# Attention with decay, then an FFN, on one core: the order of instructions planned inside the kernel

## The chip, the core and the metric

The kernel runs on one core of a Trainium2 chip. TensorE (PE) multiplies matrices into PSUM, VectorE (DVE) and ScalarE (ACT) work element by element, GpSimd (POOL) does so in SBUF only, and SyncE (SP) issues nearly all DMAs; each engine takes its instructions in a fixed order and waits on semaphores. The metric is the device time of one execution, in microseconds (us).

## The reference

```python
def _attn_ref(q, k, v, f):              # 8 batches, 8 heads, 576 positions, 64 wide
    scores = q @ k^T / sqrt(D)
    cum = np.cumsum(np.log(np.clip(f, 0.0001, 1.0)), axis=-1)
    scores = np.where(causal, -1e9, scores + cum[:, :, :, None] - cum[:, :, None, :])
    attn = softmax(scores)              # max, exp, divide by the sum + 1e-9
    return attn @ v
def _moe_ref(x, w_in, w_out):           # 4608 tokens, 512 -> 2048 -> 512
    h = x @ w_in
    g = np.where(h >= 1, h, np.where(h <= -1, 0.0, (h + 1) ** 2 / 4))
    return g @ w_out
```

x is the attention's output, with the heads of a position side by side. All data is float32.

## The kernel before

**Numbers in two halves.** A float32 operand of a large matmul is scaled by a power of two and split into two fp16 parts, high (`[.., 0, ..]`, written by ACT) and low (the rest, written by DVE, some by POOL). A product takes three fp16 matmuls: high by high, high by low, low by high. The scores pack both halves of q and k into the 128 rows and take two. The first jobs use plain float32 matmuls instead: scores up to job `NQK` = 12, values up to job `NPE` = 5.

**Jobs.** A job is a pair of heads of a batch. Batch 0 is cut in rows 0 to 255 and 256 to 575 (jobs 0 to 3 and 4 to 7), every other batch has four jobs of 576 rows; 36 in all, and 32 full pairs. Jobs 8 to 11 are batch 1, jobs 12 to 35 the 24 pairs of batches 2 to 7, which I number as pairs too (job 12 is the first). A job goes row block by row block (r = 0 to 4, 128 rows each, 64 in the last, where both heads share one tile):
- `load`, `prepare`: q and k come in; from job 12 on they are scaled and split into `qs` (L393 to L420, L420 once a pair), and a DMA transposes `qs` into `qkT`. Earlier jobs are transposed on PE (L375).
- `scores`: PE multiplies (L479 float32, L485 fp16), POOL makes the decay part from `ck` (the sums `cum_d`, broadcast to all rows) in `sdr` (four buffers) or `sd` (fifth row, two buffers) and masks it.
- `weights`: DVE adds both and takes the row's maximum (L572), ACT takes exp with the sum (L576), DVE inverts the sum, ACT and DVE write the high and low half of the weights (`pr`, L590 and L596), and SP's DMAs transpose `pr` into `pT` (L602, L605), of which there is one buffer. Up to job 4, `turn_rows` transposes on PE in float32 instead (L514, L520), with the inverse sums on a diagonal (L503).
- `values`: PE multiplies `pT` by v (L616, in float32 L545), in one run of 36 matmuls per pair, and ACT and DVE write x in two halves (L625, L626).

**v.** `split_values` loads a pair's v for its own values. Before that `value_scale` loads all of a batch's v once more, pair by pair through the `ck` buffers, for one maximum over the batch (L243 the load, L244 the reduce on DVE).

**FFN.** 18 chunks of 256 tokens by 8 blocks of the hidden width make 144 units. `moe_front` is 24 matmuls into a PSUM bank `ph` (L658, two banks), then ACT relu (L667) and square (L668), DVE max/min (L669), ACT high half (L671), DVE low half (L672); `moe_back` is 12 matmuls of 512 columns into `po` (L686). A chunk over a batch border has twice as many, narrower front matmuls. The FFN's weights arrive packed in pairs of words, are put right and split block by block in 32 pieces of 512 columns (`weight_split`, L195 to L227) during the first jobs.

**What sets the order.** The code is written job by job with quotas of FFN units in between; the framework's scheduler then orders the instructions by its own model of their times.

Of the kernel before, what the change touches and what calls it, by code (L numbers as in the profile page):

```python
# [25 lines left out]

CUTS = {0: ((0, 2), (2, 5))}

NPE = 5
NQK = 12  # L30

POOL_LOW = {6: (2, 4), 7: (2, 4)}

EARLY = ((0, 0, 3), (0, 3, 6), (0, 6, 8))

CONVERT = {1: 1, 2: 1, 3: 1, 4: 2, 5: 2, 6: 1}
LOADS = {0: 2, 1: 3}
# [9 lines left out]
def kernel(  # L47
# [10 lines left out]

# [35 lines left out]
    early = xpool.tile([P, NPAIR, 2, S], F16, name="x").rearrange("p a b s -> p (a b s)").bitcast(F32)  # L94

    xs = {b: xpool.tile([P, NPAIR, 2, S], F16, name="x") for b in range(2)}
    x1 = xs[1].rearrange("p a b s -> p (a b s)").bitcast(F32)
    stage = xs[1].rearrange("p a b s -> p (a b s)").bitcast(F32)
# [12 lines left out]

    def across(dst, m):

        n = m.shape[1]
        pt = ps.tile([P, 512], F32, name="s")
        nc.tensor.transpose(pt[0:n, 0:P], m, ident)  # L120
# [12 lines left out]

    ident = const.tile([P, P], F32, name="ident")
    make_identity(nc, ident)
    ones = const.tile([2, P], F32, name="ones")
    nc.gpsimd.memset(ones, 1.0)
    cum_d = dram.tile([B * H, S], F32, name="cum_d")
    cq = const.tile([P, NT5, B * H], F32, name="cq")

    def decay_sums():
        fl = early
        nb = B * H
        nc.sync.dma_start(fl[0:nb, 0:S], f.rearrange("b h s -> (b h) s"))
# [23 lines left out]
    wi = [place[2 * i].rearrange("p l (t c) -> p l t c", t=NKT) for i in range(NB)]  # L170
    wo = [place[2 * i + 1].rearrange("p l (t c) -> p l t c", t=2) for i in range(NB)]
    mi = const.tile([P, NB], F32, name="mi")
    mp = const.tile([P, 2, NB], F32, name="mp")
    sw = const.tile([P, 2, NB], F32, name="sw")

    def weight_load(i):
# [4 lines left out]
        for k_, slot in enumerate(RAW[i]):  # L181
            src = srcs[k_ // 2]
            n = src.shape[1] // 2
            nc.sync.dma_start(
                slots[slot].rearrange("p (t c) -> p t c", t=n), src[:, n * (k_ % 2):n * (k_ % 2 + 1), :]
            )

    def weight_split(i):
        ms = tiny.tile([P, 2, 2], F32, name="ms", bufs=2)
        wfs = []  # L190
        for k_, slot in enumerate(RAW[i]):
            top = slots[slot][:, 1::2]
            low = slots[slot][:, 0::2]
            bits = two.tile([P, DM], F32, name="u").bitcast(I32)
            nc.vector.tensor_scalar(  # L195
                out=bits, in0=top, scalar1=0x07FFFFFF, scalar2=3, op0=ALU.bitwise_and, op1=ALU.logical_shift_left
            )
            nc.vector.scalar_tensor_tensor(
                out=bits, in0=low, scalar=29, in1=bits, op0=ALU.logical_shift_right, op1=ALU.bitwise_or
            )  # L200
            nc.vector.scalar_tensor_tensor(
                out=top, in0=top, scalar=-0x40000000, in1=bits, op0=ALU.bitwise_and, op1=ALU.bitwise_or
            )
            wf = top.bitcast(F32)
            wfs.append(wf)
            m = ms[:, k_ // 2, k_ % 2:k_ % 2 + 1]
            if k_ < 0:
                nc.vector.tensor_reduce(out=m, in_=wf, axis=AX.X, op=ALU.max, apply_absolute_value=True)
            else:
                nc.scalar.activation(low.bitcast(F32), wf, AF.Abs, accum_out=m)  # L210
        m1 = tiny.tile([P, 2], F32, name="m1w", bufs=2)
        nc.vector.tensor_reduce(out=m1, in_=ms, axis=AX.X, op=ALU.max)
        m = tiny.tile([P, 2], F32, name="m2", bufs=2)
        across(m, m1)
        nc.vector.tensor_copy(mi[:, i:i + 1], m[:, 0:1])
        scale_of(sw[:, :, i], mp[:, :, i], m)
        for k_, wf in enumerate(wfs):
            j = k_ // 2
            s = sw[:, j, i:i + 1]
            c = slice(k_ % 2 * DM, (k_ % 2 + 1) * DM)  # L220
            hi, lo = place[2 * i + j][:, 0, c], place[2 * i + j][:, 1, c]
            nc.scalar.activation(hi, wf, AF.Copy, scale=s)
            if k_ < 2:
                nc.gpsimd.tensor_scalar(out=wf, in0=wf, scalar1=s, scalar2=0.0, op0=ALU.mult, op1=ALU.add)
                nc.gpsimd.tensor_tensor(out=lo, in0=wf, in1=hi, op=ALU.subtract)
            else:
                nc.vector.scalar_tensor_tensor(out=lo, in0=wf, scalar=s, in1=hi, op0=ALU.mult, op1=ALU.subtract)  # L227


    mv = const.tile([P, B], F32, name="mv")  # L230
    pv = const.tile([P, B], F32, name="pv")
    sv = const.tile([P, B], F32, name="sv")
    bsc = {}

    def value_scale(b):
        m4 = tiny.tile([P, NPAIR], F32, name="m4", bufs=2)
        for i in range(NPAIR):
# [5 lines left out]
            nc.sync.dma_start(st, part)  # L243
            nc.vector.tensor_reduce(  # L244
# [6 lines left out]
        if b:  # L251
            nc.vector.tensor_tensor(out=m, in0=m, in1=mv[:, b - 1:b], op=ALU.max)
# [590 lines left out]
```

## Time and profile before

| | us |
|---|---|
| median of three runs (1189.17 to 1194.98) | 1193.62 |
| span of the profiled execution (its whole time stands in no view; the median of the runs is 3.9 longer) | 1189.7 |
| PE busy | 1059.5 |
| VectorE busy | 816.9 |
| ScalarE busy | 804.5 |
| GpSimd busy | 452.7 |

The span runs from the first to the last instruction. Matmuls are pipelined and their modelled ends overlap, so the busy times of single lines of PE add up to more than PE's own. In a row of a view, "x" is the number of instructions, then come busy us and mean ns, and behind the bar the idle time of the engine before them with what ended it.

### The profile page before, as it was taken

The page shows a single profiled execution, that of the slowest core. Times are in us where ns is not written, and L with a number is a line of the kernel's source. Part 1 is how long each engine was busy: PE and PEld are TensorE (multiplying, and loading weights), DVE is VectorE, ACT ScalarE, POOL GpSimd, SP SyncE. Part 2 cuts the span into 40 slices and gives each one's busy share as a digit, 9 for nine tenths or more (in the row PEclk, how much of TensorE's full clock was granted, in tenths as well). Part 3 has the DMA queues.
Part 4 walks back from the last instruction along what each step waited for, and adds up shares of the span by engine and source line. Part 5 has one row for each costly group of instructions (what it writes and reads, how often), then busy time and mean ns, then how long its engine had stood idle before and what let it go on. Part 6 is the DMA issues. An engine that isn't in the chain of part 4 may idle for free. (4 is left out here: it accounts for less than half of the span.)

```text
span 1189.7 us, 24378 instructions
## 1 busy us (share of the span) xinstructions
PE 1059.5 (89%) x8553; PEld 695.6 (58%) x8553; DVE 816.9 (69%) x2327; ACT 804.5 (68%) x1698; POOL 452.7 (38%) x699
## 2 busy tenths in 40 slices
PE   4667788994889899999998999989898989999998
PEld 3444455662555566666665666656665656677665
DVE  6898886674877787778666868768866788523222
ACT  5867677773777687768775767758866687644443
POOL 5677453441554245425423225524533265000000
PEclk9778798997999999999999999999999999999999
DMA  8885466686899588968866649767978587300000
GB/s 261 251 232 134 114 144 131 132 149 137 152 161 191 110 173 158 184 137 170 168 105 134 128 85 172 153 148 149 168 134 173 116 169 110 74 19 2 18 19 18
DMA packets 439258, 160.04 MB, mean 135 GB/s; under 512 B 414944, under 2 KB 415968, under 8 KB 439136
## 3 DMA queue, kind: packets, MB, share of 16 engines
q1 hardware_dynamic: 433952, 149.05, 62.2%
q10 hardware_dynamic: 5184, 9.44, 2.4%
q8 instruction: 67, 1.10, 0.4%
q14 instruction: 55, 0.45, 0.1%
HBM read 75.64 MB, written 9.58 MB: 72 GB/s over the span
## 5 line engine op out<-in xcount | busy, mean ns | idle before, releaser
L658 PE MATMUL ph<-x,place 128*128 128x256 f16 (+3 forms) x4608 | 448.9, 248 | 30.1 <-DVE u L669 29.8
L658 PEld LDWEIGHTS <-place 128*128 128x128 f16 x4608 | 362.4, 99 | 117.0 <-issue 25.8
L686 PE MATMUL po<-place,g 128*128 128x512 f16 x1728 | 418.0, 380 | 7.5 <-DVE g L672 3.8
L686 PEld LDWEIGHTS <-g 128*128 128x128 f16 x1728 | 162.1, 98 | 169.2 <-ACT g L671 6.9
L489 POOL TENSOR_SCALAR sdr<-ck,nsig,cqs 128x128 f32<-128x128 f32 (+1 forms) x192 | 160.7, 840 | 214.7 <-DVE pr L596 142.6
L669 DVE SCALAR_TENSOR_TENSOR u<-ph,z,u 128x512 f32<-128x512 f32 x136 | 101.1, 744 | 109.8 <-ACT u L668 109.5
L576 ACT ACTIVATE sdr<-sdr,nm 128x384 f32<-128x384 f32 (+1 forms) x248 | 137.9, 557 | 49.3 <-DVE nm L572 44.0
L667 ACT ACTIVATE u<-ph,z 128x512 f32<-128x512 f32 x136 | 104.3, 767 | 80.2 <-PE ph L658 79.6
L596 DVE SCALAR_TENSOR_TENSOR pr<-sdr,rc,pr 128x384 f16<-128x384 f32 (+2 forms) x232 | 128.8, 580 | 30.2 <-ACT pr L590 29.9
L671 ACT ACTIVATE g<-u,z 128x512 f16<-128x512 f32 x136 | 97.3, 716 | 68.2 <-DVE u L669 66.1
L672 DVE SCALAR_TENSOR_TENSOR g<-u,z,g 128x512 f16<-128x512 f32 x136 | 105.1, 773 | 53.8 <-ACT g L671 53.4
L489 POOL TENSOR_SCALAR sd<-ck,nsig,cqs 64x576 f32<-64x576 f32 x48 | 53.8, 1120 | 222.6 <-DMA ck<-cum_d 84.3
L590 ACT ACTIVATE pr<-sdr,rc 128x384 f16<-128x384 f32 (+1 forms) x236 | 119.7, 556 | 14.6 <-DVE rc L587 5.0
L572 DVE CUSTOM_DVE_ANT_0 sdr<-s,sdr,nalpha 128x128 f32<-128x128 f32 (+1 forms) x192 | 102.1, 543 | 31.8 <-POOL sdr L493 18.2
L616 PE MATMUL big<-pT,vs 128*64 128x64 f16 (+3 forms) x1098 | 88.3, 285 | 30.0 <-DMA pT<-pr 28.4
L616 PEld LDWEIGHTS <-vs 128*64 128x64 f16 x1098 | 59.1, 111 | 65.8 <-issue 26.5
L493 POOL TENSOR_SCALAR_AFFINE_SELECT sdr<-sdr 128x128 f32<-128x128 f32 x248 | 91.7, 380 | 11.1
L668 ACT ACTIVATE u<-u 128x512 f32<-128x512 f32 x144 | 89.5, 622 | 2.0
L485 PE MATMUL s<-qkT 128*128 128x128 f16 (+3 forms) x384 | 78.4, 300 | 5.5 <-DVE nm L572 4.3
L393 ACT ACTIVATE qs<-qk 128x640 f16<-128x640 f32 x48 | 35.0, 729 | 58.4 <-DMA qkT<-qs 50.6
L485 PEld LDWEIGHTS <-qkT 128*128 128x128 f16 (+1 forms) x576 | 45.0, 101 | 39.9 <-issue 18.0
L489 POOL TENSOR_SCALAR sdr<-ck,cq 128x384 f32<-128x384 f32 (+3 forms) x56 | 44.8, 800 | 56.6 <-DVE pr L596 27.0
(168 smaller groups left out, 1175.0 us busy)
## 6 DMA issues: line engine op xcount, KB each, us to landing
ck<-cum_d SPq DMA_DIRECT2D x64, 288.0 KB, 4.1
out_dram<-ot ACTq DMA_DIRECT2D x36, 256.0 KB, 3.4
qk<-in_k_dram SPq DMA_DIRECT2D x64, 128.0 KB, 3.1
ck<-in_v_dram SPq DMA_DIRECT2D x28, 288.0 KB, 2.9
v<-in_v_dram SPq DMA_DIRECT2D x62, 128.0 KB, 3.5
qk<-in_q_dram SPq DMA_DIRECT2D x56, 128.0 KB, 2.6
place<-in_moe_w_in_dram SPq DMA_DIRECT2D x11, 512.0 KB, 5.3
place<-in_moe_w_out_dram SPq DMA_DIRECT2D x10, 512.0 KB, 6.0
```

The costliest lines, as they stand in the source:

```text
L485: nc.tensor.matmul(sp[p0:p1, c0:c1], lhsT=w.q[:, h, q0 - w.s0:q0 - w.s0 + p1 - p0], rhs=w.k[:, c, h, c0:c1], start=(c == 0), stop=(c == 1),)
L489: nc.gpsimd.tensor_scalar(out=sd[p0:p1, 0:wid], in0=w.ck[h][p0:p1, 0:wid], scalar1=w.nsig if w.p < NQK else w.nsig[p0:p1], scalar2=w.cqs[p ...
L572: nc.vector.tensor_tensor_reduce(out=a, in0=sp[:, 0:wid], in1=a, scale=w.nalpha, scalar=BIG, op0=ALU.add, op1=ALU.min, accum_out=nm[:, i:i ...
L576: nc.scalar.activation(a, a, AF.Exp, bias=nm[:, i:i + 1], scale=-1.0, accum_out=sm[:, i:i + 1])
L590: nc.scalar.activation(pr[:, :, 0, i, :], a, AF.Copy, scale=rc[:, i:i + 1])
L596: nc.vector.scalar_tensor_tensor(out=pr[:, :, 1, i, :], in0=a, scalar=rc[:, i:i + 1], in1=pr[:, :, 0, i, :], op0=ALU.mult, op1=ALU.subtract,)
L616: nc.tensor.matmul(av[64 * h:64 * h + 64, at + s0:at + s1], lhsT=w.vs[:, vl, h, t, :], rhs=w.pT[:, t, pl, h, s0:s1], start=(t == 0 and pi ...
L658: nc.tensor.matmul(ph[:, fi, a0:a1], lhsT=wi[fb][:, wl, t, fi * P:(fi + 1) * P], rhs=xs[b][:, t, xl, s0:s0 + a1 - a0], start=(fi == 0 and ...
L667: nc.scalar.activation(u, h, AF.Relu, scale=z.u[:, i:i + 1], bias=z.h[:, i:i + 1])
L669: nc.vector.scalar_tensor_tensor(out=u, in0=h, scalar=z.t[:, i:i + 1], in1=u, op0=ALU.max, op1=ALU.min)
L672: nc.vector.scalar_tensor_tensor(out=g[:, 1], in0=u, scalar=z.r[:, i:i + 1], in1=g[:, 0], op0=ALU.mult, op1=ALU.subtract)
L686: nc.tensor.matmul(po[ch][i], lhsT=g[:, gl, fi * TC + i * P:fi * TC + (i + 1) * P], rhs=wo[fb][:, wl, fi, :], start=(first and fi == 0 and ...
```

## The change

The whole of the kernel's body is written anew. What differs:

- **Planned order.** Each piece of work is put on a list (`Order.op`) with engine, duration, reads, writes and a priority. `Order.plan` runs through it in time and takes, on every free engine, the ready operation of the lowest priority number whose buffers are free; the kernel then emits the instructions in that order, and the framework's own scheduler is off (`manual_schedule`). The durations are formulas in the columns (`act_us`, `dve_us`, `pool_us`, `COL`). Attention of job j is held to the planned time 100 + 27 (j - 8), in the plan alone.
- **Values in two parts.** `pT` is two buffers, for rows 0 to 255 and 256 to 575 (`HALF`); values of the first part follow row block 1. Two runs of 12 and 30 matmuls take the place of one of 36.
- **Three banks.** `ph` and `s` have three PSUM banks each, where both had two and `big` had two more. Transposes on PE and the small reductions across rows (`across`) use `ph` banks, the fifth row's scores (512 and 64 columns apart, with a minimum over both) and the values use `s` banks.
- **v kept on chip.** Four resident tiles `v32` hold a batch's v; the maximum is taken from them, and the second load is gone.
- **Batch 0 in float32.** `NPE` is 8: jobs 5 to 7 take the float32 turn and values. Their diagonals, and those of jobs 0 to 4, are made on POOL (`L933`), not ACT.
- The FFN's weights go in 16 pieces of 1024 columns; the first groups of blocks are (0, 2), (2, 5), (5, 8) and the first two chunks use them; `sd` for the fifth row has one buffer.

```diff
-NPE = 5
+HALF = ((0, 256), (256, 576))
+NPE = 8
...
+GROUPS = ((0, 2), (2, 5), (5, 8))
+EARLY = ((0, 0), (0, 1), (1, 0), (1, 1), (0, 2), (1, 2))
+HOLD, PACE = 100.0, 27.0
...
+class Order:
+    def op(self, eng, dur, emit, reads=(), writes=(), prio=0.0, size=0.0, mode=0):
...
+        self.ops.append([eng, dur, emit, deps, bufs, prio, size, mode, self.hold])
...
+    def plan(self):
...
+            t = heapq.heappop(events)
...
+                for eng, l in waiting.items():
+                    if free[eng] > t + 1e-9:
+                        continue
...
+                    for i in l:
+                        if ready[i] > t + 1e-9:
+                            continue
...
+                        if ok:
+                            pick = i
+                            break
...
+                    start[i] = (t, done)
...
+        return sorted(range(n), key=lambda i: start[i])
+def act_us(n, ptr=0, acc=0):
+    return 0.18 + 0.00084 * n + (0.1 if ptr else 0.0) + (0.05 if ptr > 1 else 0.0) + 0.19 * acc
+def dve_us(n):
+    return 0.2 + 0.00107 * n
...
-    ps = ctx.enter_context(tc.tile_pool(name="ps", bufs=2, space=bass.MemoryType.PSUM))
-    ps1 = ctx.enter_context(tc.tile_pool(name="ps1", bufs=1, space=bass.MemoryType.PSUM))
+    ctx.enter_context(tc.manual_schedule())
+    s_pool = Pool([((f"s{i}",), psum.tile([P, 512], F32, name=f"s{i}")) for i in range(3)])
+    f_pool = Pool([((f"ph{i}",), psum.tile([P, 512], F32, name=f"ph{i}")) for i in range(3)])
...
+    vres = [sb([P, 2, NT5, D], F32, f"v32_{i}") for i in range(NPAIR)]
+    sd4_pool = ring("sd4_", 1, [P, SP], F32)
+    pt_pool = [ring(f"pT{i}_", 1, [P, NT5 if i else 2, 2, 2, HALF[i][1] - HALF[i][0]], F16) for i in range(2)]
...
-                st = two.tile([P, S], F32, name="ck", bufs=3)
-            part = v[b, 2 * i:2 * i + 2].rearrange("h s d -> (h s d)").rearrange("(p n) -> p n", p=P)
-            nc.sync.dma_start(st, part)
+                out=m4.ap[:, i:i + 1], in_=vres[i].rearrange("p h t d -> p (h t d)"), axis=AX.X, op=ALU.max,
...
+    for i in od.plan():
+        od.ops[i][2]()
```

How this moves instructions, at the two places that matter most below. First SP's queue before batch 2, where the maximum of that batch's v is needed (`ck` buffers, `pr` and `pT` the weights before and after transposition, `cum_d` the decay sums). Before:

```order
L243 DMA ck_2972<-in_v_dram 128x576
L602 DMA_TRANSPOSE pT_2803<-pr2_2941 128x12x128
L243 DMA ck_2975<-in_v_dram 128x576
L243 DMA ck_2978<-in_v_dram 128x576
L602 DMA_TRANSPOSE pT_2803<-pr3_3005 128x16x128
L243 DMA ck_2981<-in_v_dram 128x576
L605 DMA_TRANSPOSE pT_2803<-pr4_3020 128x10x64 x2
```

In the changed kernel:

```order
L533 DMA v32_0_91<-in_v_dram 128x4x64 x2
L536 DMA v32_0_91<-in_v_dram 64x2x64
L533 DMA v32_1_92<-in_v_dram 128x4x64 x2
L536 DMA v32_1_92<-in_v_dram 64x2x64
L1000 DMA_TRANSPOSE pT0_0_108<-pr0_100 128x4x128
L1000 DMA_TRANSPOSE pT0_0_108<-pr1_101 128x8x128
L662 DMA ck2_114<-cum_d_75 128x576
L533 DMA v32_2_93<-in_v_dram 128x4x64 x2
L536 DMA v32_2_93<-in_v_dram 64x2x64
L662 DMA ck0_112<-cum_d_75 128x576
L1000 DMA_TRANSPOSE pT1_0_109<-pr2_102 128x12x128
```

The loads that went through the `ck` buffers between the transposes of one pair's weights are gone; the loads into the resident tiles stand there instead of them and of the pair's own loads of v.

Second DVE's queue at the same place (`m4` the maxima, `sm2` and `rc` the row sums and their inverses). Before:

```order
L244 TENSOR_REDUCE m4_2971<-ck_2972 128x1
L584 TENSOR_SCALAR rc_3012<-sm2_3007 128x2
L587 RECIPROCAL rc_3012<-rc_3012 128x2
L584 TENSOR_SCALAR rc_3025<-sm2_3022 128x1
L587 RECIPROCAL rc_3025<-rc_3025 128x1
L596 SCALAR_TENSOR_TENSOR pr3_3005<-sdr_2_119,rc_3012,pr3_3005 128x4x128
L244 TENSOR_REDUCE m4_2971<-ck_2975 128x1
L596 SCALAR_TENSOR_TENSOR pr3_3005<-sdr_3_120,rc_3012,pr3_3005 128x4x128
L596 SCALAR_TENSOR_TENSOR pr4_3020<-sd4_1_122,rc_3025,pr4_3020 128x5x128
L244 TENSOR_REDUCE m4_2971<-ck_2978 128x1
L244 TENSOR_REDUCE m4_2971<-ck_2981 128x1
```

In the changed kernel, around the last of the four:

```order
L917 TENSOR_SCALAR nm2_126<-nm3_127 128x2
L921 RECIPROCAL nm2_126<-nm2_126 128x2
L902 ISA sdr0_95,nm5_129<-s2_67,sdr0_95 128x256
L902 ISA nm5_129 128x1
L547 TENSOR_REDUCE m4_0_143<-v32_3_94 128x1
L1070 SCALAR_TENSOR_TENSOR g1_118<-u0_115,z_2_157,g1_118 128x512
L1070 SCALAR_TENSOR_TENSOR g0_117<-u1_116,z_1_155,g0_117 128x512
L551 TENSOR_REDUCE m1_0_145<-m4_0_143 128x1
```

Each reduce stood among the low halves of the weights (L596) that the transposes take; now the four stand apart, with other work of DVE between them.

More of the change, by code (lines that the diff above doesn't have):

```diff
@@ L92 @@
-    ps1 = ctx.enter_context(tc.tile_pool(name="ps1", bufs=1, space=bass.MemoryType.PSUM))
[L94 to L98, printed above, removed]
+    psum = ctx.enter_context(tc.tile_pool(name="psum", bufs=1, space=bass.MemoryType.PSUM))
+    ctx.enter_context(tc.manual_schedule())
@@ new lines, with flat32 @@
+    ph_pool = Pool(f_pool.cands)
+    for x in (s_pool, f_pool):
+        x.strict = False
+    po_pool = Pool([(("po",), pos)])
+    ident = sb([P, P], F32, "ident")
+    ones = sb([2, P], F32, "ones")
+    cum_d = dram.tile([B * H, S], F32, name="cum_d")
+    cq = sb([P, NT5, B * H], F32, "cq")
+    cq8 = sb([P, NT5, 2 * H], F32, "cq8")
+    xt = [sb([P, NPAIR, 2, S], F16, f"x{i}") for i in range(3)]
+    slot_of = [(b + 1) % 3 for b in range(B)]
+    xs = [xt[i] for i in slot_of]
+    def flat32(t):
+        return t.rearrange("p a b s -> p (a b s)").bitcast(F32)
@@ L141, in decay_sums @@
+    for c, t in early_qk.items():
+        for h in range(2):
+            G(0.6, lambda t=t, h=h: nc.gpsimd.memset(t[64 - 64 * h:128 - 64 * h, h, :], 0.0), [], ["qz"], -8.5)
     def decay_sums():
@@ L180, in weight_load @@
         )
-        for k_, slot in enumerate(RAW[i]):
-            src = srcs[k_ // 2]
+        for j in range(2):
+            src, raw = srcs[j], raws[RAW[i][j]]
             n = src.shape[1] // 2
[L184 to L208, printed above, removed]
-            else:
[L210 to L225, printed above, removed]
-            else:
-                nc.vector.scalar_tensor_tensor(out=lo, in0=wf, scalar=s, in1=hi, op0=ALU.mult, op1=ALU.subtract)
@@ L257, with moe_scales @@
     class Scales:
         pass
-    def moe_scales(b, first=0, last=NB - 1, early_group=False):
+    zs = []
+    def moe_scales(b, first, last, prio):
         z = Scales()
@@ L453 @@
[L453 to L483 removed]
+        b, hp, r0, r1 = jobs[ji]
@@ L609, in values @@
-    def values(w, x):
-        av = ps1.tile([P, 1024], F32, name="big")
-        at = 512 - w.cuts[0][1] if len(w.cuts) == 2 else -w.s0
-        for t in range(w.r1):
-            for pi, (vl, pl) in enumerate(((0, 0), (1, 0), (0, 1))):
-                for i, s0, s1 in parts_of(w, t):
+                    out=x[:, n2:2 * n2], in0=vflat, scalar=sv[:, b:b + 1], in1=x[:, 0:n2], op0=ALU.mult,
+                    op1=ALU.subtract
+                )
+            V(640, vlo, vkeys(hp) + [("sv", b), (vs, 0)], [(vs, 1)], pr - 2)
@@ new lines, in attention, with values, early_av @@
+        pts = {}
+        def values(part):
+            s0_, s1_ = HALF[part]
+            n = s1_ - s0_
+            last = 1 if part == 0 else LAST
+            av = Buf(s_pool)
+            pT = pts[part]
+            x = xs[b]
+            cols = sum(n - max(P * t - s0_, 0) for t in range(last + 1))
+            def early_av():
+                fl = pT.ap.rearrange("p t l h s -> p (t l h s)").bitcast(F32)
+                pT32 = fl.rearrange("p (t h s) -> p t h s", h=2, s=n)
+                for t in range(last + 1):
+                    k1 = P if t < LAST else 64
+                    c0 = max(P * t - s0_, 0)
@@ new lines, in values @@
+            rows = range(2) if part == 0 else range(2, NT5)
+            keys = [(pT, r) for r in rows]
+            if p < NPE:
+                M(cols * COL * 4 + 0.2, early_av, keys + vkeys(hp), [av], pv_prio[part], 1)
+                sc_ = sv[:, b:b + 1]
+            else:
+                M(cols * COL * 3 + 0.2, late_av, keys + [(vs, 0), (vs, 1)], [av], pv_prio[part], 1)
+                sc_ = 1.0 / PSC
+            hi, lo = x[:, hp, 0, s0_:s1_], x[:, hp, 1, s0_:s1_]
+            xk = xkeys(b, hp, s0_, s1_)
@@ L643, in moe_front, with make, moe @@
-    def moe_front(ch, fb):
+            def make():
+                nc.vector.reciprocal(t, sv[:, b:b + 1])
+                nc.vector.tensor_tensor(out=t, in0=t, in1=sv[:, b + 1:b + 2], op=ALU.mult)
+                nc.vector.tensor_scalar(out=a, in0=a, scalar1=t, scalar2=None, op0=ALU.mult)
+            V(0, make, [("sv", b), ("sv", b + 1)], [k_ for hp in range(NPAIR) for k_ in xkeys(b, hp, S - n, S)], prio, 0.3 + 0.0003 * n * 8)
+    acc = {}
+    def moe(ch, first, last, z, prio):
         g0 = ch * TC
@@ L675, in moe_front @@
-        return ch, fb, g, z
-    ots = {}
-    def moe_back(ch, fb, g, z):
-        first, last, part = z.first == fb, z.last == fb, z.first > 0
-        if first:
-            po[ch] = [ps1.tile([P, DM], F32, name=f"po{i}") for i in range(2)]
-        for fi in range(2):
-            for i in range(2):
-                for gl, wl in ((0, 0), (0, 1), (1, 0)):
-                    nc.tensor.matmul(
-                        po[ch][i],
-                        lhsT=g[:, gl, fi * TC + i * P:fi * TC + (i + 1) * P],
-                        rhs=wo[fb][:, wl, fi, :],
-                        start=(first and fi == 0 and gl == 0 and wl == 0),
-                        stop=(last and fi == 1 and gl == 1),
-                    )
-        if not last:
-            return
-        if not part:
-            ots[ch] = [two.tile([P, DM], F32, name="ot") for i in range(2)]
+        xk = [k_ for a0, a1, b, s0 in segs for hp in range(NPAIR) for k_ in xkeys(b, hp, s0, s0 + a1 - a0)]
@@ L705, in moe_back @@
+            if last == NB - 1:
                 tok = ch * TC + i * P
-                nc.scalar.dma_start(out[tok:tok + P, :], ots[ch][i])
-    pending = []
-    def moe_unit(ch, fb):
-        pending.append(moe_front(ch, fb))
-        if len(pending) > 1:
-            moe_back(*pending.pop(0))
-    units = [(ch, fb) for ch, first, end in EARLY for fb in range(first, end)]
-    units += [(ch, fb) for ch in range(NCH) if ch not in [e[0] for e in EARLY] for fb in range(NB)]
-    groups = sorted({e[1:] for e in EARLY})
@@ L808 @@
-    while done < len(units):
-        moe_unit(*units[done])
-        done += 1
-    while pending:
-        moe_back(*pending.pop(0))
+                L(0.34, 0.26, lambda i=i, tok=tok: nc.scalar.dma_start(
+                    out[tok:tok + P, :], ot.ap[i]
+                ), [(ot, i)], [("out", ch, i)], prio, "ACT")
+    decay_sums()
+    for hp in range(NPAIR):
+        load_values(0, hp, -70.0)
+    value_scale(0, -65.0)
+    for i in range(NB):
+        weight_load(i, WLOAD[i])
+        weight_split(i, WPRIO[i])
@@ new lines, with chunks @@
+    groups = [moe_scales(0, a, e - 1, WPRIO[e - 1]) for a, e in GROUPS]
+    def chunks(lo, hi, z):
+        for ch in range(lo, hi):
+            moe(ch, 0, NB - 1, z, ch * 8)
+    done = 0
+    for ji in range(njobs):
+        b, hp, r0, r1 = jobs[ji]
+        attention(ji)
+        if b + 1 < B and r1 == NT5:
+            load_values(b + 1, hp, 10.0 * ji - 5)
+        if b == 0 and r1 == 2 and hp == NPAIR - 1:
+            done = 2
+        if hp == NPAIR - 1 and r1 == NT5:
+            if not b:
+                for ch, i in EARLY:
+                    moe(ch, groups[i].first, groups[i].last, groups[i], 8 * ch)
+            if b + 1 < B:
+                value_scale(b + 1, 10.0 * ji - 5)
+            if b:
+                join_scales(b - 1, b * 8.0 * 2 - 1e4)
+            z = moe_scales(b, 0, NB - 1, 10.0 * ji)
+            end = (b + 1) * S // TC
+            chunks(done, end, z)
+            done = end
```

1268 lines of the change are left out of this document (759 added, 509 removed).

## The prediction

> **What bounds the kernel now.** I read the page's busy times first, then the span cut into stages, the chain at the end of the run, the waits, and the timeline of the one large hole.
>
> ```profile
> PE 1059.5 (89%) x8553; PEld 695.6 (58%) x8553; DVE 816.9 (69%) x2327; ACT 804.5 (68%) x1698; POOL 452.7 (38%) x699
> ...
> PEclk9778798997999999999999999999999999999999
> ```
>
> ```profile
> 0.00:98.80 98.80, 57.86 (x247) 37.98 (x247) 81.05 (x230) 66.99 (x176) 65.67 (x92) 0.79 0.78 230
> 98.80:294.10 195.30, 160.84 (x1065) 98.75 (x1063) 140.18 (x419) 130.84 (x275) 88.43 (x140) 0.90 0.66 140
> 294.10:1038.70 744.60, 694.13 (x6061) 458.97 (x6057) 553.54 (x1625) 543.14 (x1156) 298.60 (x468) 1.00 0.76 145
> 1038.70:1189.70 151.00, 146.65 (x1190) 99.90 (x1188) 42.14 (x57) 63.53 (x91) 0.00 (x0) 1.00 0.04 15
> ```
>
> The windows give busy time of PE, PEld, DVE, ACT and POOL, then the granted clock. The cuts are mine: the first FFN matmul starts at 98.8, the first fp16 score matmul (pair 12, the first of batch 2) at 294.1, and the last values end at 1038.7. I call 0 to 294 stage A (12 jobs in float32 scores, all weights converted), 294 to 1039 stage B (24 pairs with FFN between them) and the rest stage C (FFN alone). PE is the bound in B and C. In A nobody is: PE is busy 218.7 of 294.1 us and DVE 221.2.
>
> What one FFN unit (24 `ph` and 12 `po` matmuls at 256 and 512 columns; a unit over a batch border is 48 shorter ones) costs is read from the chain in stage C:
>
> ```profile
> 1062.33 2.68 PE ph L658 x48
> 1065.01 2.59 PE po L686 x12
> ```
>
> So 2.68 + 2.59 = 5.27 us, 144 of them 759 us. No order removes that; what can go is idle PE (130 us in all) and the attention's own PE time. Next the waits (who waits for whom: us in total, times, the longest), over the span and then on PE between 99 and 294, and the timeline of the longest one:
>
> ```profile
> DVE m L244 <- DMA ck<-in_v_dram: 37.0, 25, 5.0
> ```
>
> ```profile
> PE big L616 <- DMA pT<-pr: 18.4, 2, 14.5
> ```
>
> ```profile
> 276.36 4.57 SPq L243 DMA_DIRECT2D ck<-in_v_dram  x2
> ...
> 279.82 0.75 DVE L244 TENSOR_REDUCE m<-ck 128x1 f32<-128x576 f32 x1 [1.67 <-DMA ck<-in_v_dram]
> ...
> 281.26 2.05 SPq L602 DMA_TRANSPOSE pT<-pr  x1
> ...
> 283.69 0.75 DVE L244 TENSOR_REDUCE m<-ck 128x1 f32<-128x576 f32 x1 [1.67 <-DMA ck<-in_v_dram]
> ...
> 284.86 2.53 SPq L605 DMA_TRANSPOSE pT<-pr  x2
> ...
> 288.53 0.64 PE L616 MATMUL big<-pT,vs 128*64 128x512 f16 x1 [14.53 <-DMA pT<-pr]
> ```
>
> This is the hole in slice 10: four loads of v go through three `ck` buffers, each waits for a reduce, DVE waits for each load, and the transposes of the weights stand behind them on SP. The values, and PE with them, wait 14.5 us. It happens at every batch border; later FFN work covers PE, but the attention loses the time:
>
> ```profile
> 327.39 0.48 DVE L420 COPY qs<-qs 128x1280 f16<-128x1280 f16 x1
> ...
> 352.45 0.48 DVE L420 COPY qs<-qs 128x1280 f16<-128x1280 f16 x1
> ...
> 374.59 0.49 DVE L420 COPY qs<-qs 128x1280 f16<-128x1280 f16 x1
> ...
> 390.37 0.75 DVE L244 TENSOR_REDUCE m<-ck 128x1 f32<-128x576 f32 x1 [0.36 <-DMA ck<-in_v_dram]
> ...
> 402.73 0.74 DVE L244 TENSOR_REDUCE m<-ck 128x1 f32<-128x576 f32 x1
> ...
> 418.05 0.48 DVE L420 COPY qs<-qs 128x1280 f16<-128x1280 f16 x1
> ```
>
> ```profile
> L420 DVE COPY qs<-qs x24: 439/480/882, 260.1 to 988.1; 128x1280 f16<-128x1280 f16 x24
> ```
>
> L420 runs once a pair; the last row gives its first and last start. Inside a batch pairs follow at 25.1 and 22.1 us, across the border 43.5; over the 24 pairs the mean is (988.1 - 260.1) / 23 = 31.7.
>
> **The change, part by part.** *v kept on chip.* 32 loads of 288 KB go; the reduces stay, from the resident tile, at about 0.75 us each. The four waits with the transposes behind them go. In DVE's order the four reduces for batch 2 stand at rows 411, 412, 455 and 514. What is late next: a v load needs its tile free, so it waits for the split of the pair before; that split is done ahead of that pair's softmax, so I cost it at nothing, at most the 37.0 us that DVE waits for v now.
>
> *Stage A.* PE: batch 0 wholly in float32 makes 100 float32 turning matmuls of 43 and 56 value matmuls of 26, and by the order 3.3 jobs of fp16 values before pair 12 where there were 6.5.
>
> ```profile
> 0.00:294.10 294.10, 15.71 (x76) 13.95 (x76) 0.86 0.70 170
> 0.00:294.10 294.10, 1.52 (x10) 1.16 (x10) 0.86 0.70 170
> 0.00:294.10 294.10, 9.18 (x52) 4.59 (x52) 0.86 0.70 170
> 0.00:294.10 294.10, 19.31 (x234) 13.34 (x234) 0.86 0.70 170
> ```
>
> These are the PE times in stage A of L514, L520 (turning), L545 (float32 values) and L616 (fp16 values; 36 a job). Turning: 17.2 / 43 = 0.40 us each, 57 more are 23 us. Values: 9.2 / 26 = 0.35, 30 more are 11; since the added ones are the wide kind I take 14. Less 19.3 x 3.2 / 6.5 = 9.5 for fp16 values, and less 1.3 fronts and 3 backs of FFN that the order moves behind pair 12 (16.8 and 16 now, 15.5 and 13 then), 11 us. PE is busy 218.7 + 23 + 14 - 9.5 - 11 = 235.
>
> [...]
>
> DVE: three jobs lose the low half of the weights and of v, and the conversion of the FFN weights goes in 16 pieces of 1024 columns, not 32 of 512.
>
> ```profile
> L672 DVE SCALAR_TENSOR_TENSOR g<-u,z,g 128x512 f16<-128x512 f32 x136 | 105.1, 773 | 53.8 <-ACT g L671 53.4 <-issue 0.3
> ...
> L669 DVE SCALAR_TENSOR_TENSOR u<-ph,z,u 128x512 f32<-128x512 f32 x136 | 101.1, 744 | 109.8 <-ACT u L668 109.5
> ...
> L596 DVE SCALAR_TENSOR_TENSOR pr<-sdr,rc,pr 128x512 f16<-128x512 f32 x62 | 46.8, 772 | 5.7 <-ACT pr L590 5.7
> ...
> L596 DVE SCALAR_TENSOR_TENSOR pr<-sdr,rc,pr 128x384 f16<-128x384 f32 x58 | 35.4, 638 | 18.7 <-ACT pr L590 18.6
> ...
> L448 DVE SCALAR_TENSOR_TENSOR vs<-v,sv,vs 128x640 f16<-128x640 f32 x31 | 27.7, 895 | 7.2 <-ACT vs L447 7.1
> ...
> L596 DVE SCALAR_TENSOR_TENSOR pr<-sd,rc,pr 128x640 f16<-128x640 f32 x29 | 25.6, 881 | 5.0 <-ACT pr L590 4.8
> ...
> L596 DVE SCALAR_TENSOR_TENSOR pr<-sdr,rc,pr 128x128 f16<-128x128 f32 x56 | 18.4, 357 | 1.5 <-ACT pr L590 1.3
> ```
>
> Per job, by these rows, 2 x 0.638 + 2 x 0.772 + 0.881 + 0.895 = 4.6 us, three are 13.8. From 357 ns at 128 and 772 at 512 columns the fixed part of one is about 0.22 us; 16 pieces fewer with three passes each, and 8 fewer of the low half, are 56 x 0.22 = 12.3. Neighbours overlap, so I count 0.85 of it: 221.2 - 22 = 199 us. At the 82% that DVE reaches in the first 98.8 us, that is 243 us; PE's 235 with all the idle time of A except the hole (294.1 - 218.7 = 75.4, less the 18.4 for `pT`) would be 292. ACT trades its weights' high half for copies out of PSUM, about even; the 36 diagonals go to POOL, which is busy 154 us in A and has room. I take 258, nearer DVE's end: it leaves PE 23 us without work and DVE 59, and no row shows a transfer that must take longer.
>
> *Stage B.* Now 100.2 fronts and 99 backs are 100.2 x 2.68 + 99 x 2.59 = 525 us; the other 694.1 - 525 = 169 us of busy PE are 24 pairs, 7.05 each. By the order 87.5 fronts and 89 backs stand there afterwards: 234.5 + 230.5 = 465, with the same 169 is 634. The order changes between attention and FFN 346 times on PE instead of 472, since a front is kept whole by halves and the values come in two runs; at nothing to 0.2 us a change this is 0 to 25, I take 10. Idle PE in B is 744.6 - 694.1 = 50.5 now, of which
>
> ```profile
> PE ph L658 <- DVE u L669: 23.5, 21, 3.0
> ```
>
> waits for an FFN bank; the third bank should end most of it. I leave 20 of the 50. Stage B: 634 - 10 + 20 = 644 us, 26.8 a pair. On DVE 12.5 units less (L669 and L672, 1.5 us together, 19 in all) and what the splits add (the x write, the fifth row's scores with a minimum; some 0.75 us a pair at 0.22 each, 18 in all) cancel: 553 us, 86% of 644, so DVE is close behind. The single buffer for the fifth row, where two were, is held by some eight steps of about a microsecond each (an estimate from the widths in the rows above), 8 of the 26.8 us, and costs nothing while rows of one pair follow those of the last.
>
> *Stage C.* 41 fronts and 42 backs remain where 27 and 29 did: 41 x 2.68 + 42 x 2.59 = 218.7, and 151.0 - 147.5 = 3.5 for the end: 222 us.
>
> Sum: 258 + 644 + 222 = 1124, against a span of 1189.7; with the 3.9 us by which the median of the runs (1193.62) exceeds that span, 1128 us.
>
> **The rivals.** *PE saturated.* If PE idles only at the start, A is 240, B 610 and C 222, with 3.9 outside 1076. For it: inside batches pairs already follow at 22 to 25 us with the same engines. Against: DVE would be busy 91% of B; it was 74%.
>
> *DVE and ACT bind the pairs (slower).* One softmax row goes DVE, ACT, DVE, ACT, DVE, and all queues are in order. If DVE stays at 74% of B as now (553.5 of 744.6), B is 553 / 0.743 = 744, the total 258 + 744 + 222 + 4 = 1228. It turns slower when B exceeds 1193.6 - 4 - 222 - 258 = 710, that is 29.6 us a pair. Against it: the 74% hold the border stalls, which go.
>
> *The gain is given back in A.* If the order leaves the float32 jobs on PE with the old idle time (A 292) and B keeps its 50 us of idle (674), the total is 1192: no change. An order written from durations that do not hold here would look so.
>
> **How the numbers follow.** Forecast (1095 to 1170) 0.66; PE saturated 0.14; given back 0.10; DVE and ACT bind 0.10. The range is 1068 to 1190: just below the saturated rival's sum at the low end, nearly all of the given-back case at the high end, the slower one outside. About 0.5% (6 us) is what a measurement can tell from no change: faster 0.85, same 0.05, slower 0.10; half of the given-back case lies below 1187.6.
>
> **What would show it.** Right: no wait of DVE for a load of v; pT waits of PE under 5 us each; the first fp16 scores near 258 us; once-a-pair copies at an even 26 to 28 us; last values near 902; then FFN alone for 222. Wrong: pairs at 30 us, first scores after 280, or PE waiting on the SP queue's transposes as before.

## The result, and the profile after

| | before | after |
|---|---|---|
| median (lowest to highest of four runs), us | 1192.62 (1189.17 to 1194.98) | 1155.39 (1154.18 to 1157.65) |
| span of the profiled execution | 1189.7 | 1154.2 |
| PE busy, PE idle | 1059.5, 130.2 | 1062.0, 92.2 |

The ratio is 0.970, with a 95% interval of 0.9663 to 0.9736: 37 us faster, where 65 were forecast. Busy times and granted clock of the changed kernel, from its page, and below them its stages by windows with the same cuts (first fp16 score matmul at 279.7, end of the last values at 931.0):

```profile
PE 1062.0 (92%) x8805; PEld 711.8 (62%) x8805; DVE 838.1 (73%) x2340; ACT 799.8 (69%) x1667; POOL 426.6 (37%) x713
...
PEclk9679998899999999999999999999999999999999
```

```profile
0.00:279.70 279.70, 225.02 (x1299) 143.51 (x1299) 219.72 (x596) 179.11 (x386) 148.00 (x242) 0.89 0.57 148
279.70:931.00 651.30, 618.57 (x5618) 416.97 (x5620) 554.91 (x1660) 526.05 (x1144) 278.63 (x472) 1.00 0.84 156
931.00:1154.20 223.20, 218.43 (x1892) 151.29 (x1888) 63.50 (x85) 94.62 (x138) 0.00 (x0) 1.00 0.04 15
```

PE's busy time is the same to 3 us; what went is 38 us of its idle time. A lost 21 of its 75 idle us, B 18 of its 50. A is still the stage in which no engine is full: PE is busy 80% of it, DVE 79%.

The waits that the prediction named are gone or small. This is what is left of DVE's wait for v, up to the last values, and then PE's longest waits in stage B:

```profile
DVE m L547 <- DMA v<-in_v_dram: 7.4, 9, 3.0
```

```profile
PE s L791 <- DVE nm L902: 12.0, 26, 1.1
PE s L791 <- DVE x L859: 5.4, 6, 2.0
PE s L791 <- DMA qkT<-qs: 4.9, 4, 1.6
PE s L842 <- DVE nm L902: 4.3, 6, 1.2
...
PE s L842 <- DMA pT<-pr: 0.9, 1, 0.9
```

37.0 us for v became 7.4, and the transposes of the weights cost PE 0.9 us instead of 28.4 over the run. No front waits for a bank in B any more. What is left are short waits for a bank that DVE still reads (`nm` is its row maximum). The once-a-pair copy:

```profile
L774 DVE COPY qs<-qs x24: 478/491/874, 271.1 to 890.2; 128x1280 f16<-128x1280 f16 x24
```

(890.2 - 271.1) / 23 = 26.9 us a pair, against 31.7 before.

### The profile page after: what moved, and what is told of

Same layout as the page of the kernel before. It is cut to its first block, busy times and chain, and to the rows that moved or that the text cites. A ratio compares the mean times of both kernels' runs of the same rounds, so it can differ in the third digit from the quotient of the medians.

```text
span 1154.2 us, 24696 instructions
## 1 busy us (share of the span) xinstructions
PE 1062.0 (92%) x8805; PEld 711.8 (62%) x8805; DVE 838.1 (73%) x2340; ACT 799.8 (69%) x1667; POOL 426.6 (37%) x713
## 5 line engine op out<-in xcount | busy, mean ns | idle before, releaser
L1051 PE MATMUL ph<-x,place 128*128 128x256 f16 (+3 forms) x4608 | 407.8, 247 | 5.2 <-DVE x L859 2.4
L1051 PEld LDWEIGHTS <-place 128*128 128x128 f16 x4608 | 356.6, 98 | 58.7 <-issue 12.7
L880 POOL TENSOR_SCALAR sdr<-ck,sg,cqs 128x128 f32<-128x128 f32 (+1 forms) x192 | 153.7, 800 | 273.2 <-DVE pr L988 213.0
L911 ACT ACTIVATE sdr<-sdr,nm 128x512 f32<-128x512 f32 (+3 forms) x246 | 135.9, 553 | 45.9 <-DVE nm L902 45.0
L985 ACT ACTIVATE pr<-sdr,nm 128x128 f16<-128x128 f32 (+1 forms) x224 | 114.9, 554 | 41.2 <-ACT sdr L911 14.0
L988 DVE SCALAR_TENSOR_TENSOR pr<-sdr,nm,pr 128x128 f16<-128x128 f32 (+1 forms) x224 | 118.4, 560 | 2.9 <-ACT pr L985 2.2
L791 PE MATMUL s<-qkT 128*128 128x128 f16 (+5 forms) x576 | 93.5, 297 | 23.5 <-DVE nm L902 12.0
L902 DVE CUSTOM_DVE_ANT_0 sdr<-s,sdr,sg 128x128 f32<-128x128 f32 (+1 forms) x192 | 100.7, 544 | 8.1 <-POOL sdr L884 4.2
L707 PE MATMUL s<-qkT 128*128 128x128 f32 (+5 forms) x192 | 65.4, 505 | 9.4 <-DVE nm L902 6.0
L842 PE MATMUL s<-pT,vs 128*64 128x320 f16 (+4 forms) x1176 | 67.9, 263 | 6.5 <-DVE nm L902 4.9
L880 POOL TENSOR_SCALAR sd<-ck,sg,cqs 64x576 f32<-64x576 f32 x48 | 44.0, 918 | 73.1 <-DVE pr L988 60.9
```

Of the source, the lines that this page charges most:

```text
L791: nc.tensor.matmul(sp[p0:p1, 0:c1 - c0], lhsT=tq[:, h, q0 - s0:q0 - s0 + p1 - p0], rhs=tk[:, c, h, c0:c1], start=(c == 0), stop=(c == 1),)
L842: nc.tensor.matmul(av.ap[64 * h:64 * h + 64, c0:n], lhsT=vs.ap[:, vl, h, t, :], rhs=pT.ap[:, t, pl, h, c0:n], start=(t == 0 and pi == 0), ...
L880: nc.gpsimd.tensor_scalar(out=sd.ap[p0:p1, 0:wid], in0=cks[h].ap[p0:p1, 0:wid], scalar1=ns if p < NQK else ns[p0:p1], scalar2=cqs()[p0:p1, ...
L911: A(wid, lambda i=i, sd=sd, wid=wid, nm=nm, sm=sm: nc.scalar.activation(sd.ap[:, 0:wid], sd.ap[:, 0:wid], AF.Exp, bias=nm.ap[:, i:i + 1], ...
L985: A(cols, lambda i=i, prv=prv, rows_=rows_, rc=rc: nc.scalar.activation(prv()[:, :, 0, i, :], rows_(), AF.Copy, scale=rc.ap[:, i:i + 1]), ...
L988: V(cols, lambda i=i, prv=prv, rows_=rows_, rc=rc: nc.vector.scalar_tensor_tensor(out=prv()[:, :, 1, i, :], in0=rows_(), scalar=rc.ap[:, i ...
```

## The experiments

Every edit makes the whole order be planned again, so two kernels that differ in one line differ in thousands of places. That gives each comparison a play beside the runs' own scatter, and not a small one: e5, e6, e7, e10 and e12 have the pieces of the changed kernel in another planned order, and their medians go from 1154.6 to 1179.0. The kernel before, timed beside each, went from 1192.6 to 1196.6. I therefore compare by the stages, by PE's busy and idle time, and by the FFN fronts that stand in PE's order ahead of the first fp16 score ("fronts in A"; one front with its back is 5.27 us of PE). All later verdicts rest on this table, worked out from each profile's windows; idle is length less PE's busy time.

| | median | length of A | PE idle in A | PE idle in B and C | PE busy | fronts in A |
|---|---|---|---|---|---|---|
| before | 1192.6 | 294.1 | 75.4 | 54.8 | 1059.5 | 16.8 |
| after | 1155.4 | 279.7 | 54.7 | 37.5 | 1062.0 | 15.5 |
| e1 `NPE` 5 | 1151.9 | 272.5 | 73.9 | 32.9 | 1039.8 | 14.5 |
| e2 two `ph` banks | 1180.4 | 274.4 | 66.5 | 39.3 | 1071.1 | 11.5 |
| e3 framework's order | 1195.7 | 277.7 | 56.4 | 66.2 | 1072.3 | 16 |
| e4 v through `ck` | 1151.4 | 275.6 | 59.4 | 33.8 | 1058.7 | 13.5 |
| e5 values in one go | 1154.8 | 285.0 | 59.0 | 31.5 | 1063.0 | 15.5 |
| e6 no hold | 1170.8 | 274.4 | 61.2 | 40.0 | 1071.0 | 12 |
| e7 measured costs in A | 1175.4 | 279.4 | 66.1 | 36.6 | 1072.5 | 13 |
| e8 low halves on POOL | 1170.5 | 285.6 | 69.0 | 37.2 | 1062.7 | 13 |
| e9 weights not packed | 1134.2 | 239.2 | 45.7 | 33.4 | 1052.6 | 12 |
| e10 FFN part held back | 1179.0 | 280.3 | 72.3 | 34.0 | 1074.6 | 10 |
| e11 e1 and e4 | 1155.8 | 284.2 | 67.1 | 28.6 | 1057.3 | 14.5 |
| e12 `PACE` 28 | 1154.6 | 279.9 | 58.7 | 32.2 | 1063.2 | 14.5 |

**e3: the same pieces, the framework's order.**

```diff
-    ctx.enter_context(tc.manual_schedule())
```

> The changed kernel's pieces (buffers, banks, resident v, float32 batch 0, values in two parts) with the framework's own scheduler switched on again, which orders the instructions anew by its own model. If the planned order carries the gain, the time goes back to the level before or above it: 1190 to 1240, idle PE in stage B back to 50 us or more. Rival: the pieces carry it (no border stalls, third bank), and the order is worth little: 1150 to 1170.

Ratio to before 0.9998 (0.9969 to 1.0026). Stage B and PE's waits in it:

```profile
277.70:974.00 696.30, 634.80 (x5636) 418.13 (x5634) 540.95 (x1653) 517.54 (x1146) 288.58 (x475) 0.98 0.78 145
```

```profile
PE s L790 <- DVE nm L901: 16.0, 13, 3.4
PE s L790 <- DMA qkT<-qs: 14.8, 12, 2.6
```

Third bank, resident v, two values parts and float32 batch 0 are all in it, and it is as slow as before. Its 40 us over the changed kernel lie in B: 29 of idle PE and 16 of busy PE (for 18 more matmuls), less 4 elsewhere. The gain needs the planned order. It isn't the luck of one plan either: all planned kernels here have 28.6 to 40.0 us of idle PE in B and C, the two in the framework's order 54.8 and 66.2, and no run of the same pieces in a planned order was slower than 1182.6, none of e3 faster than 1188.2. How the old pieces would do in a planned order was not run.

**e2: two `ph` banks.**

```diff
-    f_pool = Pool([... for i in range(3)])
+    f_pool = Pool([... for i in range(2)])
```

> The changed kernel with two ph banks instead of three; the eighth PSUM bank stays empty and the order is planned anew for that. The prediction gave the third bank about 23 us in stage B (the wait of front matmuls for DVE's u) and some of the 118 changes on PE. By it: B 670 to 685, the whole 1170 to 1185, and the wait of front matmuls for u is back near 20 us. Rival: a planned order keeps FFN and attention out of each other's way with two banks as well; the whole within 8 us of 1155.

Ratio 0.987 (0.9841 to 0.9899): 25 us slower than the changed kernel. Over the whole run fronts wait for a bank again (6.6 us of it in B, where 23.5 stood before):

```profile
PE ph L1051 <- DVE u L1064: 15.6, 13, 3.7
```

But PE idles in B only 2 us more than after, and B, 665.7 us, missed the 670 to 685. What is lost is 12 us of idle time in A and 9 of busy time; four fronts fewer are done in A, and C is 236.8 us long. e7 and e10 lose 20 and 24 us in the same way with three banks, by the order alone. So this run doesn't show what the bank itself is worth.

**e4: the maximum of v loaded through `ck` again.**

```diff
+            st = Buf(ck_pool)
+            L(0.5, 0.29, lambda i=i, st=st: nc.sync.dma_start(st.ap, v[b, 2 * i:2 * i + 2]...), [], [st], prio)
-                out=m4.ap[:, i:i + 1], in_=vres[i]...
+                out=m4.ap[:, i:i + 1], in_=st.ap, axis=AX.X, op=ALU.max, apply_absolute_value=True,
```

> The changed kernel with the maximum of v taken from a second load through the ck buffers again, as before; the resident tiles and the rest stay, and the order is planned anew with these loads in it. If the loads of v at the batch borders cost the attention 10 to 18 us each as read from the profile before, and that delay cannot be covered now that PE is nearly full: the pairs across a border 37 to 43 us apart, the whole 1175 to 1195. Rival: with the loads placed by the plan the border costs little, since FFN covers PE: the whole 1153 to 1163, pairs across a border within 6 us of the others.

Ratio 0.9619 (0.9584 to 0.9654), no slower; the interval lies just below that of the changed kernel, to which e11 comes back. The border stalls are back: pairs across four borders are 41 to 48 us apart, across the fifth 34, other pairs 19 to 34. Stages B and C:

```profile
275.60:963.80 688.20, 659.17 (x6068) 447.93 (x6068) 563.90 (x1678) 542.83 (x1170) 280.28 (x472) 1.00 0.81 157
963.80:1151.90 188.10, 183.35 (x1488) 125.06 (x1488) 52.97 (x71) 77.97 (x114) 0.00 (x0) 1.00 0.04 15
```

B is 37 us longer, with 450 more matmuls, and C 35 shorter: PE does FFN units while the attention stalls, and these are then missing at the end.

**e12: a slower pace.**

```diff
-HOLD, PACE = 100.0, 27.0
+HOLD, PACE = 100.0, 28.0
```

> PACE 28 for 27: each pair of batches 1 to 3 may start 1 us later than the pair before it did, 23 us in all by the last. Theory 1, the time is TensorE's work and its idle time, and the attention's pace costs nothing while FFN units fill the gaps: stage B longer by 10-35 us, C shorter by about as much, 1150-1162 us. Theory 2, the attention's pace is in the time, as the prediction had it with its 26.8 us per pair: 1170-1180 us.

Ratio 0.9646 (0.9615 to 0.9677).

```profile
279.90:960.50 680.60, 653.41 (x5985) 444.26 (x5983) 566.38 (x1680) 541.43 (x1170) 284.46 (x474) 1.00 0.80 151
960.50:1154.10 193.60, 188.57 (x1548) 128.93 (x1546) 54.41 (x73) 80.11 (x117) 0.00 (x0) 0.99 0.04 15
```

B is 29.3 us longer, C 29.6 shorter. Theory 1 holds: at this pace the attention's speed isn't in the time.

**e6: no hold at all.**

```diff
-        od.hold = max(0.0, HOLD + PACE * (ji - 8))
+        od.hold = 0.0
```

> The changed kernel planned without the hold of job j to 100 + 27 (j - 8): attention, which goes ahead of the FFN, runs as fast as VectorE and ScalarE let it. Theory: the time is PE's work plus its idle time, so only what stands beside the attention counts. Without the hold attention is denser, fewer fronts (under 80 instead of 87.5) stand in stage B, PE waits more for VectorE there, and the idle time of B grows from 33 to 45 or more: the whole 1165 to 1190. Rival: stage A was held up by the hold; then A falls under 265 and the whole under 1148.

Ratio 0.9802 (0.9778 to 0.9826): 15 us worse, within the theory's range, but not for its reason: B idles 35.0 us, not 45. A is 5 us shorter, so the hold isn't what makes it long. Without the hold 12 fronts stand in A, PE idles 6.5 us more there, and C is 236.9 us. A slower pace in B is free; attention that comes ahead of FFN units in A was not.

**e5: values in one go, e1: `NPE` 5.**

```diff
-        pv_prio = (pr + 2.5, pr + 11.5)
+        pv_prio = (pr + 2.5 if r1 == 2 else pr + 11.5, pr + 11.5)
...
-            if r == 1:
-                values(0)
+        if r0 == 0:
+            values(0)
```

> The changed kernel with both runs of a full pair's values after its last row block, planned anew; pT stays in two buffers. If the early first part matters (it frees its pT buffer and breaks up a run of 42 matmuls), the transposes of the next pair wait for it: stage B longer by 10 to 25 us, the whole 1165 to 1180. Rival: PE always has FFN to do meanwhile, so the two parts are worth nothing: 1150 to 1161, as moving the loads of v was.

Ratio 0.9675 (0.965 to 0.97): the two parts, computed one behind the other, are worth nothing that shows.

```diff
-NPE = 8
+NPE = 5
```

> The changed kernel with NPE = 5: jobs 5 to 7 of batch 0 take the fp16 weights and values again. Stage A (up to the first fp16 scores) came out at 279.7 us where 258 were forecast; two theories for the 22 us. Theory DVE: VectorE is the bound of A (219.7 us busy, where 199 were forecast). Then the low halves of three jobs, about 3 x 4.6 us, come back on it: A 285 to 295, the whole 1160 to 1172. Rival, float32 on PE: PE's slow float32 matmuls at 0.6 to 0.9 of the clock (about 48 us of turning and values in A) hold A up. Then A falls by 10 to 25 us and the whole is 1130 to 1148.

Ratio 0.9628 (0.9585 to 0.967); the interval overlaps that of the changed kernel. PE has 26 us less to do in A and idles 19 more; A is 7 shorter, although DVE has 7 us more to do there (227.1). So neither theory's range came, and DVE's busy time alone does not set A. Float32 for all of batch 0 brings nothing that shows.

**e7 and e8: two ideas on stage A that fell.**

```diff
-            passes = 4
+            passes = 4 * 1.29
...
-            ), key, [bits], prio)
+            ), key, [bits], prio, 1.47)
```

> The changed kernel with the plan's durations for stage A set to what its own trace shows there: float32 scores 1.29 times, float32 turns 0.33 instead of 0.26 us a block, float32 values 1.22 times, the passes of the weight conversion 1.47 to 1.57 us instead of 1.3. If stage A is 22 us over its forecast because the order rests on durations that do not hold at the lower clock, A falls to 255 to 270 and the whole to 1130 to 1146. Rival: A is as long as the work on PE and VectorE makes it, in any order: A 272 to 285, the whole 1150 to 1160.

Ratio 0.9841 (0.9809 to 0.9872), A 279.4. Truer durations for A's float32 work and conversions don't shorten it, so these durations are not what makes it long; the new order has fewer fronts in A and is 20 us slower, with the same pieces and the same instructions.

```diff
-            if j == 0:
+            if j < 2:
                 G(1.4, lambda wf=wf, s=s: nc.gpsimd.tensor_scalar(
```

> The changed kernel with all low halves of the FFN weights made on GpSimd (two instructions of some 1.4 and 2.6 us a piece) instead of half of them on VectorE, planned anew. VectorE loses 8 instructions of 1.4 us, 11 us, in stage A; GpSimd, busy 148 of 280 us there, gets 32. If VectorE sets A: A 262 to 270, the whole 1140 to 1149. Rival: A is set by the chain of jobs and PE at its low clock: A within 5 us of 280, the whole 1150 to 1160.

Ratio 0.9799 (0.9772 to 0.9826), A 285.6. DVE lost 2 us in A and POOL gained 25; the first front starts at 80.9 instead of 58.6. That fits slower passes on POOL (two of 1.2 and 2.4 to 2.5 us a piece in the changed kernel, where VectorE's one takes 1.35 to 1.46) delaying the weights themselves, but e4's first front starts at 81.0 too, with A at 275.6; it was not tried apart.

**e9: what holds stage A.**

```diff
-            V(0, lambda ...: nc.vector.tensor_scalar(... op0=ALU.bitwise_and, op1=ALU.logical_shift_left ...
-            V(1024, lambda ...: nc.vector.scalar_tensor_tensor(... op0=ALU.logical_shift_right, op1=ALU.bitwise_or ...
-            V(1024, lambda ...: nc.vector.scalar_tensor_tensor(... op0=ALU.bitwise_and, op1=ALU.bitwise_or ...
```

> Leaves out the three VectorE passes that pack a float64 weight into a float32 (716, 1445 and about 1500 ns each, 16 times: 58 us of VectorE in stage A); the upper words are used as weights. Planned anew, it has 12 FFN fronts in stage A against 15.5. Theory 1, VectorE sets the length of stage A: its 219.7 us there fall to about 162 and A from 279.7 to 225-245. Theory 2, something else sets A (the chain of the eight row blocks, or the planned order itself): A stays at 265-285, and the 3.5 fewer units come back as about 18 us in stage C: 1155-1175 us. By theory 1 with those units lost: 1120-1140 us.

Ratio 0.9485 (0.9461 to 0.9508), 1134.19 us.

```profile
0.00:239.20 239.20, 193.49 (x1168) 124.66 (x1169) 156.25 (x535) 169.65 (x374) 132.13 (x243) 0.91 0.68 170
239.20:922.50 683.30, 654.73 (x5911) 440.68 (x5912) 566.54 (x1679) 542.19 (x1169) 280.46 (x471) 1.00 0.82 151
922.50:1131.70 209.20, 204.38 (x1728) 140.51 (x1726) 58.91 (x79) 86.28 (x126) 0.00 (x0) 1.00 0.04 14
```

Both numbers of theory 1 came: with 63.5 us less on DVE, A is 40.5 shorter. No other edit brought A under 272, and fewer fronts alone don't (e10 has 10 of them and A at 280.3). So the packing of the weights on VectorE is what holds stage A most. Whether by its load on VectorE or by the time until a block's weights are ready stays open, since this run takes both away; the first front starts at 57.3, hardly before the 58.6 of the changed kernel. With the packing gone DVE is at 65% and PE at 81% there, and what binds then I did not test. The time fell by 21 only: the rest of A's 40 is FFN work that now stands in B and C (their sum is 18 us longer).

**e10: FFN later.**

```diff
                 for ch, i in EARLY:
+                    od.hold = 260.0 if i == 2 else 0.0
                     moe(ch, groups[i].first, groups[i].last, groups[i], 8 * ch)
```

> The last FFN part (blocks 5 to 7 of the first two token chunks) is held back to 260 us of the plan, so that stage A has 10 fronts against 15.5; nothing else changes. Theory 1, A has a length of its own and every unit not done there comes back behind the attention at 5.27 us: A 272-286, C longer by about 29 us, 1178-1190 us. Theory 2, the FFN units in A hold up its row blocks on TensorE: A falls by up to 29 us to about 251 and the time stays at 1150-1160 us.

Ratio 0.9863 (0.9834 to 0.9891): 24 us slower, A 280.3. Theory 1: A keeps its length, PE idles in it, and the units come back, 14 us of them in B and 12 in C.

**e11: e1 and e4 together.** The diff is that of both.

> Both edits that came out 4 us faster alone: NPE = 5 and the maximum of v through the ck buffers. Theory 1, those 4 us are parts that add up: 1146-1150 us. Theory 2, they are the luck of one plan against another, and another plan lies anywhere within some 6 us of the changed kernel: 1149-1161 us.

Ratio 0.9674 (0.9637 to 0.9711). The two 4 us don't add up; theory 2. So e1 and e4 are not shown to be faster than the changed kernel, and no other version with the whole computation was.

## Why the prediction was right or wrong, by its steps

- **The whole, 1128 forecast, 1155.4 measured.** The direction and the mechanism, idle PE that goes, were right; the gain is 37 us of the 65. The sum held 46.5 us of idle PE and 1078 busy, and 92.2 and 1062.0 came. So idle PE was taken 46 us too low, and 16 us of PE's work that did not come hid a third of that, which was luck. Of the signs, the first fp16 scores came at 279.7, at the edge of the 280 that was to mean wrong, and the last values at 931 for 902; PE's waits for `pT` and stage C came as said.
- **Stage A, 258 forecast, 279.7 measured: the mis-sized term.** I took PE 235 and DVE 199 busy, with 23 us of idle PE. PE came out lower, 225.0: turning and float32 values take 33 and 15 us by their rows, where 40 and 23 stood in my sum. DVE came out at 219.7, hardly below the 221.2 of before. The passes on 1024 columns saved about what was said (their rows add up to 68.7 us, 80.0 before, 11.3 for 12.3). The low halves of the weights and of v lost 9.4 of the 13.8 us: 9 rows of the weights left A, not 15. The 40 pairs of instructions for the sums' inverses cost 18.3 us for 15.0, and the minimum over the two parts of the fifth row, which I had not counted in A, 3.1, as these rows show (before, then after, both in stage A):

```profile
L584 DVE TENSOR_SCALAR rc<-sm 128x2 f32<-128x2 f32 (+1 forms) x29 | 5.9, 205 | 3.9 <-ACT sdr L576 3.7 <-ACT sd L576 0.2
L587 DVE RECIPROCAL rc<-rc 128x2 f32<-128x2 f32 (+1 forms) x29 | 4.6, 160 | 0.6
...
L579 DVE TENSOR_SCALAR rc<-sm 128x2 f32<-128x2 f32 (+1 forms) x11 | 3.0, 288 | 0.9 <-ACT pr L576 0.6 <-ACT sdr L576 0.2
...
L580 DVE RECIPROCAL rc<-rc 128x2 f32<-128x2 f32 (+1 forms) x11 | 1.5, 148 | 0.0
```

```profile
L917 DVE TENSOR_SCALAR nm<-nm 128x2 f32<-128x2 f32 (+1 forms) x40 | 11.7, 293 | 11.1 <-ACT sdr L911 5.8 <-ACT pr L911 3.3 <-ACT sd L911 2.0
...
L921 DVE RECIPROCAL nm<-nm 128x2 f32<-128x2 f32 (+1 forms) x40 | 6.6, 166 | 1.4
...
L907 DVE TENSOR_TENSOR nm<-nm 128x1 f32<-128x1 f32 x8 | 3.1, 390 | 0.2
```

  All rows together fell by 16 us (259.5 to 243.5) where I had 26. Their overlap shrank from 38.3 to 23.8 us, so only 1.5 reached the busy time: the factor 0.85 was no constant. At the 82% that I used, 219.7 would have given 268; it was 79%. For the lean towards DVE's end speaks e9; against DVE's load alone speaks e1, where A is shorter with more of it.
- **Stage B, 644 forecast, 651.3.** PE's busy 618.6 less the 465 us of FFN is 153.6, so the steadier order saved 15 us, not 10 (e3, with the same pieces and nearly the same matmuls in B, has 634.8). No row shows the 0.2 us a change that I had as a bound; 15 us over 126 changes would be 0.12 each. Idle was 32.7, not 20. The bank wait went as said, but the third bank isn't why B idles less: with two banks B idles 34.5 us (e2), with three in the framework's order 61.5 (e3).
- **Stage C, 222 forecast, 223.2.** The count of units from the order was enough.
- **v kept on chip.** The waits for v shrank from 37.0 to 7.4 us and the pairs came at 26.9 us, as said (not evenly: 20 to 36). That a border loss costs time was wrong: e4 brings the losses back at no cost. The step "later FFN work covers PE, but the attention loses the time" should have ended with "and the time is PE's". Only in the hole of slice 10 did PE run dry, and its 14.5 us were a small part of the 130 that PE idled.
- **The rivals.** "Given back in A" came half true: 22 of its 34 us. "PE saturated" was 40 us short in A and 41 in B; its 610 for B lay below the 624 us of work in my own sum, and needed all of the 25 us for changes of order. "DVE and ACT bind the pairs" did not come: DVE is at 85% of B, and e12 shows that pairs a microsecond slower would have cost nothing as long as FFN units fill in, so its price of one for one was also wrong.
- **Outside the span** 1.2 us of the median against 3.9. The 3.9 set the median of some runs against the span of another: run by run the kernel before is 1.9 to 2.4 us longer than its own span, the changed one 1.8 to 1.9.
- **The clock.** A's granted clock rose from 0.86 to 0.89, and PE was busy less than forecast. That the added float32 work did this is not shown: e1, without that work, has 0.89 in A too, e11 0.84. In one stretch a lower clock does stand beside more idle PE. Between 240 and 280 us, the changed kernel (0.96, PE busy 36.41 us) and then e10 (0.72, 24.17 us), which has no front and a single back to put there:

```profile
240.00:280.00 40.00, 36.41 (x279) 23.78 (x276) 35.65 (x112) 28.53 (x60) 16.47 (x29) 0.96 0.67 137
```

```profile
240.00:280.00 40.00, 24.17 (x136) 12.09 (x136) 31.00 (x111) 22.79 (x54) 17.55 (x34) 0.72 0.61 127
```

  A window's busy share alone doesn't give the clock, though: from 220 to 240 us e10 is granted 1.00 with PE busy 13.86 of 20 us.

## What to carry to other kernels

Where one engine has work in reserve that fits anywhere, price a stall by whether that engine runs dry, not by how long the stage gets: border stalls of about 15 us and a pace 1 us slower per pair cost nothing that shows here, while the 5.5 FFN units that e10 put off from the poorly filled first stage cost 24 us. With the new buffers and tiles in place, the planned orders that I ran were 17 to 41 us faster than the framework's; the new buffers and tiles without a planned order brought nothing. When an order is planned anew by every edit, the plan alone can move the time by more than 20 us (e7, e10), so a difference of 4 us says nothing on the edit, and one of 15 to 25 only where the stages show where it lies and why.

## What the runs showed of the hardware that I had not expected

In one stretch where PE has more gaps, some of its matmuls are longer too. In e10's last 40 us of A the granted clock is 0.72 where PE is busy 60%, against 0.96 at 91% in the changed kernel from 240 to 280 us. By the two timelines, from first start to last end, two float32 score matmuls with 512 columns take 2.07 us there for 1.02 and 1.12, and a run of 30 fp16 value matmuls 3.25 for 1.75, while four of the FFN's with 512 columns take 1.03 in both. Over the run this does not add up to a rule. The eleven kernels with the same 8805 matmuls have PE busy from 1052.6 us (e9, 79 us idle) to 1074.6 (e10, 106 us idle), but e8 idles 106 us as well and is busy 1062.7. How much of PE's busy time the clock makes is not settled.
